# Attention and expert kernel on one core: the first pair's smallest scores get a visit and a load of their own, and the order is chosen anew

## The chip, the core and the metric

The kernel runs on one core of one Trainium2 chip. A core has TensorE for matrix products, which write to PSUM banks, VectorE, ScalarE and GpSimd for work on elements, and SyncE, which like ScalarE issues transfers (DMA). Each engine works through its own queue in order and waits on semaphores for the others. The metric is the time of one execution on the device in microseconds. The kernel before takes 539.85 us, the median of 3 runs (539.78 to 540.04).

## The reference

Local causal attention and a read from a memory are mixed by a gate for each head; the result goes through a two-layer network with a squared ReLU. B = 4, H = 8, S = 576, D = 64; 2304 tokens of 512 values, 2048 hidden units.

```python
scores = scale * q @ k.T            # causal, then softmax
local = softmax(scores) @ v
q_p = phi(q)                        # phi(x) = where(x > 0, x, exp(x) - 1) + 1
mem_out = (q_p @ M_prev) / ((q_p * z_prev).sum(-1) + 1e-6)
g = sigmoid(beta)                   # one for each head
attn = g * mem_out + (1 - g) * local
h = x @ w_in                        # x: attn, heads side by side
out = (s * relu(h) ** 2 + b) @ w_out
```

## The kernel before

Two heads make a pair; the sixteen pairs go through attention one after the other. The 576 queries of a head are cut into five tiles, 0 to 4 (the first has 64 rows, the others 128), whose causal widths are 64, 192, 320, 448 and 576 columns (`QW`). For each pair:

- SyncE loads q and k transposed (`load_qk`), q in rows (`qs`), z and the values with the memory (`V`). For pair 0 the q and k columns come in the chunks of `CHUNKS0`, and ScalarE's queue loads a second copy of q's first 64 columns.
- TensorE computes scores in visits, groups of tiles that share a buffer (`SCORES`, for pair 0 `SCORES0`). The buffers are `SB`, two tiles of two banks each, pool "S", and `TB`, four tiles of one bank, pool "T". A 32-bit product shows as two passes in the trace.
- VectorE adds the mask and takes the minimum (`red`, line 377), ScalarE exponentiates with a running sum (`ex`, line 383), VectorE inverts the sums, GpSimd or VectorE scales (`scale`, line 389). `phi` makes the memory's side from `qs`: ReLU and exponential on ScalarE, products with z on GpSimd or VectorE, and two `put`s (line 318) into the probabilities' tile `P`.
- TensorE transposes `P` in four banks (`bank`, line 468), ScalarE or VectorE copies them to `F` and `pt` (`copy`, lines 477 to 484), and TensorE multiplies by `V` (`second`, line 520). ScalarE and VectorE split the result into high and low parts (`xs`, `x4`, lines 541 and 542).

Between these stand the conversion of the weights w_in (`xa` to `w0H`, `w0L` and so on, lines 564 to 579) and, as soon as a batch's four pairs are there, the first layer's products (`mm1`, lines 586 to 588). When the pairs are through, the rest of the first layer and the whole second layer run on TensorE.

What sets the order: every step is added to a `Plan` with an engine, a cost, a rank and the pools that it takes and gives back. `ORDER` is a table with one number for each step; `deal` sorts each engine's steps by it, plays the queues against the costs, and emits the steps by their planned starts. `waits` then puts dummy products (`warm`) on the identity wherever the plan leaves TensorE a gap; `setup` puts `WARM` of them on zeros at the very start (line 247). Letters in tables choose an engine for each pair or tile: `RELU`, `ZMUL`, `PUTS`, `COPY`, `SCAL`, `HIGH`, `LOW`, `QL` (A ScalarE, D VectorE, P GpSimd). `HOME` chooses the pool for each early first-layer product. gin holds the gate's beta on its way through the sigmoid (lines 640 to 647), omg its complement.

## Time and profile before

| | before |
|---|---|
| median of 3 runs | 539.85 us |
| the profiled execution's own time | 539.81 us |
| its span, first to last instruction | 538.0 us |
| TensorE busy | 529.4 us, 98% |
| VectorE, ScalarE busy | 408.0 us, 405.6 us |
| GpSimd busy | 265.0 us |
| transfers | 81.51 MB |

The span is the time between the first and the last instruction of the program; what lies around it makes up the rest of the execution's time. Busy time is a union over an engine's instructions. An idle time that stands in brackets behind a row is the engine's wait just before the instruction, with the instruction that ended it. Instructions of one engine overlap a little where the next is taken up before the last has drained, so what an instruction costs its queue is read from its start to the next start. The ends of matrix products are modelled; their starts are recorded.

### The profile page before, as it was taken

To read this page: it belongs to the slowest core of one execution; us is meant where nothing else is said; L and a number is where in the kernel's file an instruction comes from. 1 tells how busy PE (TensorE), PEld (TensorE's weight loads), DVE (VectorE), ACT (ScalarE), POOL (GpSimd) and SP (SyncE) were. 2 spreads that over 40 slices of the span, in tenths; PEclk is the share of its full clock that TensorE was granted. 3 is DMA by queue.
4 is the path that set the end of the run, shared out by engine and by line. 5 is a ranking of instruction groups with operands and counts; after the bars stand their busy time and mean duration, and the time that the engine had idled before them with its cause. 6 is when DMAs were issued, how large, how long until landed. Compare 5 with 4: busy or idle time off the path is not lost.

```text
span 538.0 us, 11590 instructions
## 1 busy us (share of the span) xinstructions
PE 529.4 (98%) x4156; PEld 444.1 (83%) x4156; DVE 408.0 (76%) x1000; ACT 405.6 (75%) x895; POOL 265.0 (49%) x264
## 2 busy tenths in 40 slices
PE   8989999999999999999999999999999999999997
PEld 6767777777888778777788888899999998998996
DVE  5999999999877766545339897436798889889773
ACT  6999999988999546455336578879987887897840
POOL 3999544365784514121000000517768768768760
PEclk9999999999999999999999999999999999999999
DMA  7666668665514513212176756466353353452101
GB/s 224 183 174 188 231 213 256 210 175 190 160 67 143 182 62 114 78 60 84 40 277 239 252 193 214 147 217 195 115 169 110 122 176 95 141 163 90 39 30 40
DMA packets 56666, 81.51 MB, mean 152 GB/s; under 512 B 7584, under 2 KB 39072, under 8 KB 56608
## 3 DMA queue, kind: packets, MB, share of 16 engines
q1 hardware_dynamic: 54064, 78.63, 45.2%
q10 hardware_dynamic: 2544, 2.14, 1.2%
q8 instruction: 33, 0.54, 0.4%
q14 instruction: 25, 0.20, 0.1%
HBM read 57.15 MB, written 23.59 MB: 150 GB/s over the span
## 4 chain that ended last, share of the span: by engine, by line
PE 91%; ACT 6%; DVE 2%; DMA 1%; issue 0%; ACTq 0%; DVEq 0%
PE yps L868 12%; PE yps L872 11%; PE sb L520 7%; PE tb L586 7%; PE tb L587 6%; PE tb L588 6%; PE hps L586 5%; PE hps L587 5%; PE hps L588 5%; PE tb L468 5%; PE yps L871 5%; PE yps L870 5%; PE sb L364 4%; PE sb L370 2%; ACT P L383 2%; PE sb L586 2%
## 5 line engine op out<-in xcount | busy, mean ns | idle before, releaser
L383 ACT ACTIVATE P<-P,mn 128x64 f32<-128x64 f32 (+4 forms) x160 | 90.2, 571 | 15.2 <-DVE mn L377 15.2
L872 PE MATMUL yps<-rb,op 128*128 128x256 f32 x360 | 101.1, 281 | 0.0
L389 POOL TENSOR_SCALAR P<-P,sr,omg 128x192 f32<-128x192 f32 (+4 forms) x112 | 80.0, 726 | 36.0 <-ACT r L609 16.1
L377 DVE CUSTOM_DVE_ANT_0 P<-sb,mask 128x64 f32<-128x64 f32 (+4 forms) x160 | 73.1, 481 | 15.8 <-PE sb L364 12.8
L868 PE MATMUL yps<-rb,op 128*128 128x512 f32 x216 | 76.9, 396 | 0.0
L872 PEld LDWEIGHTS yps<-rb,op 128*128 128x128 f32 x360 | 67.9, 189 | 0.0
L848 POOL TENSOR_TENSOR sum<-src 128x512 f32<-128x512 f32 x10 | 12.9, 1294 | 104.3 <-ACT src L832 89.6
L856 POOL TENSOR_TENSOR op<-src,op 128x512 fp32r<-128x512 f32 x30 | 43.7, 1477 | 18.7 <-ACT op L855 18.6
L879 DVE TENSOR_TENSOR yu<-yu,yps 128x256 f32<-128x256 f32 x90 | 36.5, 414 | 20.3 <-PE yps L872 19.2
L868 PEld LDWEIGHTS yps<-rb,op 128*128 128x128 f32 x216 | 40.6, 188 | 9.0
L468 PEld LDWEIGHTS tb<-ident,P 64*128 64x128 f32 x928 | 36.1, 139 | 8.8 <-issue 4.1
L468 PE MATMUL tb<-ident,P 64*128 64x64 f32 x928 | 41.1, 226 | 1.6 <-DVE xs L542 0.7
L870 PE MATMUL yps<-rb,op 128*128 128x256 f32 x144 | 40.5, 281 | 0.0
L871 PE MATMUL yps<-rb,op 128*128 128x256 f32 x144 | 40.5, 281 | 0.0
L855 ACT CAST op<-src 128x512 fp32r<-128x512 f32 x50 | 30.4, 616 | 11.7 <-PE yps L872 8.8
L856 DVE TENSOR_TENSOR op<-sum,op 128x512 fp32r<-128x512 f32 x36 | 36.7, 1021 | 0.3 <-ACT op L855 0.2
L856 POOL TENSOR_TENSOR op<-w1H,op 128x512 fp32r<-128x512 f32 x24 | 34.9, 1481 | 0.0
L383 ACT ACTIVATION_READ_ACCUMULATOR P<-P,mn 128x1 f32 x160 | 32.8, 205 | 0.0
L370 PE MATMUL sb<-qk 64*128 64x288 f32 (+4 forms) x192 | 30.7, 415 | 1.9 <-DVE mn L377 1.7
L593 ACT ACTIVATE r<-hps 128x256 f32<-128x256 f32 x62 | 21.9, 386 | 13.5 <-DMA r_d<-r 9.4
L586 PE MATMUL tb<-xs,w0H 128*128 128x512 f32 x76 | 31.4, 413 | 0.0
L855 ACT CAST op<-sum 128x512 fp32r<-128x512 f32 x36 | 22.3, 619 | 11.9 <-PE yps L872 6.8
(177 smaller groups left out, 1618.5 us busy)
## 6 DMA issues: line engine op xcount, KB each, us to landing
r_d<-r SPq DMA_DIRECT2D x41, 256.0 KB, 2.4
src<-r_d SPq DMA_DIRECT2D x20, 512.0 KB, 4.5
qk<-in_qk_t_dram SPq DMA_DIRECT2D x15, 576.0 KB, 4.7
raw<-in_moe_w_out_dram SPq DMA_DIRECT2D x16, 512.0 KB, 6.5
w1H<-r_d SPq DMA_DIRECT2D x16, 512.0 KB, 4.5
xa<-in_moe_w_in_dram SPq DMA_DIRECT2D x12, 512.0 KB, 4.9
r_d<-r SPq DMA_DIRECT2D x48, 128.0 KB, 1.8
qs<-in_q_rows_dram SPq DMA_DIRECT2D x16, 320.0 KB, 3.4
```

Source lines behind the costliest of these rows:

```text
L377: nc.vector.tensor_tensor_reduce(P[:, j, PB[i] + 64:PB[i] + 64 + n], at(ps, j, o, n), m, -SCALE, 3.0e38, ALU.add, ALU.min, mn[:, j, i:i + 1])
L383: nc.scalar.activation(pt, pt, AF.Exp, scale=-1.0, bias=mn[:, j, i:i + 1], accum_out=sm[:, j, i, 0:1])
L389: e.tensor_scalar(pt, pt, sr[:, j, i:i + 1], omg[:, h:h + 1], ALU.mult, ALU.mult)
L468: nc.tensor.transpose(TB[ps[h]][:, o[h]:o[h] + 64], P[rs, j, c:c + 128], ident[rs, rs], tile_position=(64 * h, 0))
L586: nc.tensor.matmul(ps, lhsT=wH[:, p, fs], rhs=xs[:, 0], start=p == 0, stop=False)
L587: nc.tensor.matmul(ps, lhsT=wH[:, p, fs], rhs=xs[:, 1], start=False, stop=False)
L588: nc.tensor.matmul(ps, lhsT=wL[:, p, fs], rhs=xs[:, 0], start=False, stop=p == NP - 1)
L856: (nc.gpsimd if m in ONPOOL else nc.vector).tensor_sub(L, x, H.bitcast(F32))
L868: nc.tensor.matmul(tile, lhsT=H, rhs=B, start=f == 0, stop=False)
L870: nc.tensor.matmul(ps, lhsT=H, rhs=B[:, 0], start=f == 0, stop=False)
L871: nc.tensor.matmul(ps, lhsT=H, rhs=B[:, 1], start=False, stop=False)
L872: nc.tensor.matmul(ps, lhsT=L, rhs=B[:, 0], start=False, stop=f == KF - 1)
```

## The change

- `SCORES0` gives tile 0 of pair 0 a visit of its own, ahead of tile 1's. This visit takes two "T" banks, one for each head, and not an "S" buffer; `at`, `scores` and `red` get the pool as an argument for that. Each bank is given back by its own head's reduction.
- `CHUNKS0` gets a first chunk of 64 columns; the next 128 columns (64 to 192) are loaded from ScalarE's queue instead of SyncE's, behind the second copy of q's first 64 columns. gin's load, first on that queue before, now comes behind both.
- `WARM` goes from 7 to 6 products.
- The sums of tiles 0 and 1 are still inverted together, after tile 1's visit (`parts`).
- The tables of letters, `HOME` and `ORDER` are replaced. Pair 0's two puts go from VectorE to GpSimd.

```diff
 SCORES0 = (
-    ((0, 0, 64, 0), (1, 0, 192, 64)),
+    ((0, 0, 64, 0),),
+    ((1, 0, 192, 0),),
     ((2, 0, 320, 0),),
-CHUNKS0 = ((0, 192), (192, 448), (448, 576))
+CHUNKS0 = ((0, 64), (64, 192), (192, 448), (448, 576))
...
-    WARM, FILL = 7, (0, 0, 0, 0)
+    WARM, FILL = 6, (0, 0, 0, 0, 0)
...
-    PUTS = "DDPPDPDDPPPPPPPD"
+    PUTS = "PDPPPPDDPPPPPDPD"
...
         def load_qk(a, z):
-            nc.sync.dma_start(both[:, :, a:z], qk_t[b, p][:, :, a:z])
+            (nc.scalar if g == 0 and a == 64 else nc.sync).dma_start(both[:, :, a:z], qk_t[b, p][:, :, a:z])
...
-        def at(ps, j, o, n):
+        def at(ps, j, o, n, pool):
+            if pool == "T":
+                return TB[ps[j]][:, o:o + n]
             return SB[ps[j]][:, o:o + n] if len(ps) == 2 else SB[ps[0]][:, 512 * j + o:512 * j + o + n]
...
+            small = g == 0 and v == 0
+            pool = "T" if small else "S"
...
-            wide = v == len(visits) - 1
+            wide = small or v == len(visits) - 1
...
     ORDER = [
-        (one number for each step)
+        (one number for each step)
     ]
```

What the tables of letters and `ORDER` do is told by the engines' queues. ScalarE from its first instruction, before; `qk_106` holds pair 0's q and k, `P_120` its probabilities:

```order
L640 DMA gin<-in_beta_dram 128x8
L349 DMA qk_106<-in_qk_t_dram 128x64
L641 ACT_TABLE_LOAD
L641 ACTIVATE omg<-omg 128x8
L644 ACTIVATE gin<-gin 128x8
L383 ACTIVATE P_120,sm_116<-P_120,mn_114 128x64
L383 ACTIVATE P_120,sm_116<-P_120,mn_114 128x192
```

And now:

```order
L351 DMA qk_106<-in_qk_t_dram 128x64
L341 DMA qk_106<-in_qk_t_dram 128x2x128
L646 DMA gin<-in_beta_dram 128x8
L647 ACT_TABLE_LOAD
L647 ACTIVATE omg<-omg 128x8
L387 ACTIVATE P_120,sm_116<-P_120,mn_114 128x64 x2
L650 ACTIVATE gin<-gin 128x8
L387 ACTIVATE P_120,sm_116<-P_120,mn_114 128x192 x2
```

Two loads of q and k stand ahead of gin's, and gin's exponential stands between those of tile 0 (64 columns) and tile 1 (192 columns).

TensorE from its first product, before:

```order
L247 MATMUL tb_101<-xa 128x128 x7
L370 MATMUL sb_96<-qk_106 128x64 x2
L370 MATMUL sb_96<-qk_106 128x192 x2
L370 MATMUL sb_97<-qk_106 128x320 x2
L370 MATMUL sb_96<-qk_106 128x448 x2
```

And now:

```order
L248 MATMUL tb_101<-xa 128x128 x6
L374 MATMUL tb_98<-qk_106 128x64
L374 MATMUL tb_99<-qk_106 128x64
L374 MATMUL sb_96<-qk_106 128x192 x2
L374 MATMUL sb_97<-qk_106 128x320 x2
L374 MATMUL sb_96<-qk_106 128x448 x2
```

Tile 0's two scores have moved from the buffer that they shared with tile 1 to a bank each, and one product on zeros is gone.

ScalarE between the third pair's second product, whose result the casts of `xs` and `x` read, and the fourth pair's copies to `pt` and `F`, before; `P_120` now holds the fifth pair, `P_121` the fourth:

```order
L383 ACTIVATE P_120,sm_116<-P_120,mn_114 128x64
L566 ACTIVATE xa<-xa 128x256
L383 ACTIVATE P_121,sm_117<-P_121,mn_115 128x576
L295 ACTIVATE phr<-qs_110 128x640
L383 ACTIVATE P_120,sm_116<-P_120,mn_114 128x448
L541 CAST x_137<-tb_100 128x64
L541 CAST xs<-tb_101 128x256
L566 ACTIVATE xa<-xa 128x256
L541 CAST xs<-tb_100 128x256
L477 COPY pt<-tb_98 128x8x64
```

And now:

```order
L387 ACTIVATE P_120,sm_116<-P_120,mn_114 128x448
L387 ACTIVATE P_120,sm_116<-P_120,mn_114 128x192
L547 CAST x_137<-tb_100 128x64
L547 CAST xs<-tb_100 128x256
L547 CAST xs<-tb_99 128x256
L387 ACTIVATE P_120,sm_116<-P_120,mn_114 128x320
L572 ACTIVATE xa<-xa 128x256
L387 ACTIVATE P_120,sm_116<-P_120,mn_114 128x64
L581 CAST w0H<-xa 128x256
L483 COPY pt<-tb_98 128x8x64
```

Of the fifth pair's exponentials, two stood ahead of the fourth pair's copies, of 64 and 448 columns; now there are four, with one of 192 and one of 320.

## Rows read from the trace of the kernel before

**Rows 1.** Stretches: length, busy us (instructions) of PE, PEld, DVE, ACT, POOL; clock, DMA.

```profile
0.00:6.26 6.26, 4.98 (x26) 4.25 (x26) 0.89 (x7) 1.70 (x4) 2.08 (x12) 1.00 0.56 156
6.26:53.37 47.11, 43.41 (x492) 31.84 (x490) 45.55 (x182) 47.08 (x141) 40.67 (x55) 1.00 0.66 198
53.37:57.00 3.63, 3.57 (x37) 2.15 (x33) 3.63 (x11) 3.63 (x14) 0.98 (x1) 1.00 0.87 323
57.00:262.00 205.00, 205.00 (x1866) 159.87 (x1865) 156.84 (x484) 156.82 (x415) 91.18 (x107) 1.00 0.44 141
```

**Rows 2.** Timeline, 0.7 to 8 us, all engines: start us, us, engine, line, instruction.

```profile
0.72 1.34 SPq L340 DMA_DIRECT2D qk<-in_qk_t_dram  x2
0.73 0.39 ACTq L640 DMA_DIRECT2D gin<-in_beta_dram  x1
1.04 3.35 PE L247 MATMUL tb<-xa 128*128 128x128 f32 x14 [1.04 <-DVE omg L251]
1.16 0.44 ACTq L349 DMA_DIRECT2D qk<-in_qk_t_dram  x1
...
3.44 0.21 ACT L644 ACTIVATE gin<-gin 128x8 f32<-128x8 f32 x1 [0.30 <-DMA gin<-in_beta_dram]
...
4.64 1.67 PE L370 MATMUL sb<-qk 64*128 64x64 f32 x12 [0.25 <-DMA qk<-in_qk_t_dram]
...
5.93 0.22 DVE L377 CUSTOM_DVE_ANT_0 P<-sb,mask 128x64 f32<-128x64 f32 x1 [1.84 <-PE sb L370]
...
6.26 0.35 ACT L383 ACTIVATE P<-P,mn 128x64 f32<-128x64 f32 x1 [2.61 <-DVE mn L377]
...
6.91 1.02 PE L370 MATMUL sb<-qk 64*128 64x448 f32 x4 [0.61 <-DVE mn L377]
...
7.98 0.62 DVE L377 CUSTOM_DVE_ANT_0 P<-sb,mask 128x448 f32<-128x448 f32 x1 [0.30 <-PE sb L370]
```

**Rows 3.** Line 247: engine, operation, count, duration in ns (least, median, most), first and last start.

```profile
L247 PE MATMUL tb<-ident x38: 275/275/377, 7.9 to 43.7; 128*128 128x128 f32 x38
```

**Rows 4.** Timelines of TensorE, ScalarE and GpSimd, 50 to 54 us.

```profile
50.54 0.71 PE L468 MATMUL tb<-ident,P 64*128 64x64 f32 x16 [0.18 <-POOL P L318]
...
52.57 1.08 PE L370 MATMUL sb<-qk 64*128 64x320 f32 x7
53.71 0.76 PE L520 MATMUL tb<-F,V 128*64 128x320 f32 x4
...
51.77 1.23 ACT L479 COPY F<-tb 128x512 f32<-128x512 f32 x2
52.73 0.54 ACT L484 COPY F<-tb 128x256 f32<-128x256 f32 x1
53.00 0.65 ACT L481 COPY F<-tb 128x384 f32<-128x384 f32 x1
...
51.04 0.78 POOL L318 TENSOR_TENSOR P<-qs,nrm 128x256 f32<-128x256 f32 x1
```

**Rows 5.** Loads of q and k: queue, count, KB each, median us to landing.

```profile
qk<-in_qk_t_dram SPq DMA_DIRECT2D x1, 128.0 KB, 4.2
qk<-in_qk_t_dram ACTq DMA_DIRECT2D x1, 32.0 KB, 3.3
```

**Rows 6.** Groups by shape, TensorE, 4.5 to 6.4 us: busy us, mean ns, idle before.

```profile
L370 PE MATMUL sb<-qk 64*128 64x64 f32 x4 | 0.7, 437 | 0.2 <-DMA qk<-in_qk_t_dram 0.2
```

**Rows 7.** Timeline of ScalarE, 6.6 to 9.8 us.

```profile
6.60 0.44 ACT L383 ACTIVATE P<-P,mn 128x192 f32<-128x192 f32 x1
...
7.04 0.33 ACT L383 ACTIVATE P<-P,mn 128x64 f32<-128x64 f32 x1
...
9.21 0.55 ACT L383 ACTIVATE P<-P,mn 128x320 f32<-128x320 f32 x1
...
9.75 0.55 ACT L383 ACTIVATE P<-P,mn 128x320 f32<-128x320 f32 x1
```

**Rows 8.** Timeline of GpSimd, its first work on pair 0.

```profile
10.24 1.54 POOL L305 TENSOR_TENSOR phr<-qs,z 128x640 f32<-128x640 f32 x1 [7.47 <-DVE sr L440]
```

More of the change, by code (lines that the diff above doesn't have):

```diff
@@ L272, in attention_moe_kernel @@
     RSR, WL = 0.6, 3
-    RELU = "AAAAAAAADADAAADP"
-    ZMUL = "PPPDDPDDDDPPDDDD"
-    PUTS = "DDPPDPDDPPPPPPPD"
-    COPY = ["AAAD", "AAAD", "AAAA", "AAAA", "AAAA", "AAAA", "AAAA", "AADA", "ADAA", "AAAA", "DAAA", "DDAD", "DDDA", "ADAD", "ADAA", "ADDA"]
-    SCAL = ["PPPPP", "PPPPP", "PPPPP", "PPPPP", "PPPPD", "DPPPD", "PPDPD", "PPPDP", "PPPDP", "DPPPP", "PPPDP", "PDDDP", "PDDPD", "DPDPD", "PPDPP", "DDDDD"]
-    HIGH, LOW = "PPAPAAPPAAAAAAAAAAPA", "PDPDDPPDDDPDPDDPDDDD"
-    QL = "DDDDDDDDPDDPPPPD"
+    RELU = "AAAAAAAADAAADDAD"
+    ZMUL = "PPPDDPDDDPPPDDDP"
+    PUTS = "PDPPPPDDPPPPPDPD"
+    COPY = ["AAAD", "AAAD", "AAAA", "AAAA", "AAAA", "AAAA", "AAAA", "AADA", "DDAA", "AAAA", "DAAD", "DAAA", "AAAA", "DADA", "ADAA", "DDAA"]
+    SCAL = ["PPPPP", "PPPPP", "PPDPP", "PPPPP", "PPPPD", "PPDPP", "DPPPD", "PPPDD", "DPPDP", "DPPPP", "DPPPP", "PDDPD", "DDDDD", "PDPDD", "DPDPD", "PDPDD"]
+    HIGH, LOW = "APPAPAPAAAAAAAAAAAAA", "PDPDDDPDDDPDPDDPDDDD"
+    QL = "DDDDDDDDPDPPPDPD"
     PARTS = "3232332223222222"
@@ L345, in attention @@
         for v, (a, z) in enumerate(chunks):
-            add("SP", 0.9 if g else 0.6, lambda a=a, z=z: load_qk(a, z), (r0 if g else 0) - 4.0 + 0.01 * v, writes=[("qk", u, v)],
-                bytes=(400000, 190000, 200000)[v] if g == 0 else 380000 if g == 1 else 128 * 8 * (z - a) + 32768, slack=2 if g else 1)
+            on = "ACT" if g == 0 and v == 1 else "SP"
+            add(on, 0.9 if g else 0.45 if v == 1 else 0.6, lambda a=a, z=z: load_qk(a, z), (r0 - 4.0 if g else -9.5 if v == 1 else 0) + 0.01 * v, writes=[("qk", u, v)],
+                bytes=(130000, 130000, 230000, 200000)[v] if g == 0 else 380000 if g == 1 else 128 * 8 * (z - a) + 32768, slack=(2 if g else 1) if on == "SP" else 0)
         if g == 0:
@@ L350, in attention, with scores @@
         phi(g)
-        def at(ps, j, o, n):
+        def at(ps, j, o, n, pool):
+            if pool == "T":
+                return TB[ps[j]][:, o:o + n]
             return SB[ps[j]][:, o:o + n] if len(ps) == 2 else SB[ps[0]][:, 512 * j + o:512 * j + o + n]
         fast = g >= FAST
-        def scores(group, ps):
+        def scores(group, ps, pool):
             for i, c0, n, o in group:
@@ L370, in scores, with red @@
                     nc.tensor.matmul(
[L371 removed]
+                        at(ps, j, o, n, pool), lhsT=qk[rs, 128 * i:128 * i + 128], rhs=qk[rs, S + 64 + c0:S + 64 + c0 + n],
                         start=True, stop=True, tile_position=(64 * j, 0))
[L374 removed]
+        def red(i, j, o, ps, pool):
             n = QW[i]
@@ L377, in red @@
             nc.vector.tensor_tensor_reduce(
-                P[:, j, PB[i] + 64:PB[i] + 64 + n], at(ps, j, o, n), m, -SCALE, 3.0e38, ALU.add, ALU.min,
+                P[:, j, PB[i] + 64:PB[i] + 64 + n], at(ps, j, o, n, pool), m, -SCALE, 3.0e38, ALU.add, ALU.min,
                 mn[:, j, i:i + 1])
@@ L414, in attention @@
                 cost = sum(n + 32 for _, _, n, _ in group) / 800 + 0.05
-            add("PE", cost, lambda group=group, ps=ps: scores(group, ps), r,
-                [(x, u, k) for x in ("qh", "ql") for k in range(2)] if fast else [("qk", u, k) for k in range((1, 2, 2, 3)[v] if g == 0 else 1)] + [("qk", 0, "d")] * (g == 0),
-                [("sc", g, v), "visit"], take=[(ps, "S")] * (2 if v == len(visits) - 1 else 1), mode="row")
-            wide = v == len(visits) - 1
+            add("PE", cost, lambda group=group, ps=ps, pool=pool: scores(group, ps, pool), r,
+                [(x, u, k) for x in ("qh", "ql") for k in range(2)] if fast else [("qk", u, k) for k in range((1, 2, 3, 3, 4)[v] if g == 0 else 1)] + [("qk", 0, "d")] * (g == 0),
+                [("sc", g, v), "visit"], take=[(ps, pool)] * (2 if small or v == len(visits) - 1 else 1), mode="row")
+            wide = small or v == len(visits) - 1
             if g == 0 and FILL[v]:
@@ L426, in attention @@
                     last = k == len(tiles) - 1 and (wide or j == 1)
-                    add("DVE", RED[i], lambda i=i, j=j, o=o, ps=ps: red(i, j, o, ps), r + 0.1 + 0.01 * k - UR,
+                    add("DVE", RED[i], lambda i=i, j=j, o=o, ps=ps, pool=pool: red(i, j, o, ps, pool), r + 0.1 + 0.01 * k - UR,
                         [("sc", g, v)] + ([("rd", g, v, h, q) for h in ((j,) if wide else range(2)) for q in range(len(tiles))] if last else []),
-                        [("p", u, i, j), ("mn", u, i, j), ("rd", g, v, j, k)], give=[(ps, j if wide else 0, "S")] if last else ())
+                        [("p", u, i, j), ("mn", u, i, j), ("rd", g, v, j, k)], give=[(ps, j if wide else 0, pool)] if last else ())
                     add("ACT", EXP[i], lambda i=i, j=j: ex(i, j), r + 0.15 + 0.01 * k, [("mn", u, i, j)],
@@ L630, in attention_moe_kernel @@
     LEFT = 7
-    HOME = "TTTTTTTTTTSTTTTTTTTTTTSSSTTTTTTTTTTTSTSSS"
+    HOME = "TTTTTTTTTTSTTTTTTTTTTTSTSTTTTSSTTTTTSTSSS"
     JOIN = "b0b00000b000a0bb"
```

6 lines of the change are left out of this document (2 added, 4 removed), and 102 rows, old and new, of the table ORDER.

## The prediction

> **What bounds the kernel now.** I read the stretches first [rows 1]. From 57 to 262 us TensorE is busy 205.00 of 205.00 us, and what follows is the second half of the network on the same engine. So nothing that the first pairs do can be won back after 57 us: what is early or late there moves the end by as much. The idle time of TensorE lies ahead of that point: 6.26 - 4.98, 47.11 - 43.41 and 3.63 - 3.57, together 5.04 us. Products without use fill part of what would be further gaps: 14 passes on zeros (7 products of two passes) from 1.04 us [rows 2] and 38 on the identity [rows 3].
>
> The second column to read is ScalarE. From 6.26 us, where it starts its first exponential, to 53.37 us, where it has issued the last copy of the fourth pair, it is busy 47.08 of 47.11 us [rows 1]. VectorE (45.55) and GpSimd (40.67) have gaps there. So the head of the kernel is one ScalarE queue with a start time and a length. The fourth pair's second product (line 520) starts at 53.71 us: 0.06 us after the visit ahead of it has ended, and 0.71 us after the last copy began, which takes 0.65 [rows 4]. That start is the milestone. Ahead of it TensorE has the same useful work in both orders; behind it the same again, with 71 changes between row-tiled, column-tiled and full products in either order. The time of the kernel is then the milestone plus a constant.
>
> Profiled, the kernel took 539.81 us (span 538.0); the median of the runs is 539.85, 0.04 more. I add to 539.81.
>
> **The start.** Today [rows 2]: the zero products run from 1.04 to 4.39 us; the first scores wait for q and k until 4.64; VectorE's first reduction starts at 5.93, the first exponential at 6.26, 0.33 later. Three edits move this.
>
> Dummies: 14 passes take 3.35 us, 0.239 each, so 12 end near 1.04 + 2.87 = 3.91. That is the earliest start of the scores.
>
> Loads: the second copy of q's first 64 columns, 32 KB, leaves ScalarE's queue at 0.73 instead of 1.16 [rows 2], as gin's load now comes last there. It landed 3.3 us after its issue [rows 5] and released the scores; moved by 0.43 it lets them start at 4.21. The other load that they need shrinks from 192 columns to 64. Between 3.91 and 4.64 (no gain) I take 4.1, nearest to the shifted copy, a little ahead of it because fewer bytes share the engines with it.
>
> Own visit: today's first reduction reads a tile that the matmuls of tiles 0 and 1 write, with one wait for all of them. Now tile 0 has two banks to itself, and the reduction needs only the four 64-column passes, busy 0.7 us [rows 6]. The hand-over I take from the 448-column visit: it ends at 6.91 + 1.02 = 7.93, its reduction starts at 7.98 [rows 2], 0.05 us. New: 4.1 + 0.70 + 0.05 = 4.85, + 0.33 = **5.18 for the first exponential, 1.08 us earlier**. The ends: 3.91 gives 4.99 (1.27 earlier), 4.64 gives 5.72 (0.54 earlier).
>
> Here a rule speaks against the edit of the loads. The row: SyncE spends 1.34 us on issuing its first two loads [rows 2], so a load moved to ScalarE's queue can spare the next one some 0.67 us of issue; that the issue sets the landing no row shows. The Trainium skill, page "DMA: Bandwidth & Descriptors", section "Issuing engines are not separate DMA queues", says that loads started from several engines run on the same 16 DMA engines and interleave, and that issuing from more of them saves only the time of issue. By it my 0.11 us for fewer bytes beside the copy would be void, since the same bytes follow at once from the other queue, and the sum below would be 540.03 instead of 539.92.
>
> **The ScalarE queue.** Now its length to the milestone. I counted what stands ahead of the fourth pair's last copy in each order. Copies, casts, conversions and the 64-, 448- and 576-column exponentials agree in number. The new order has three instructions more: gin's exponential, which today runs at 3.44 in idle time (0.21 us [rows 2]) and now stands between those of tiles 0 and 1; and a 192- and a 320-column exponential of the fifth pair, which today come after the copies. From start to next start a 192 takes 0.44 us (6.60 to 7.04), a 320 takes 0.54 (9.21 to 9.75) [rows 7]. Sum 0.21 + 0.44 + 0.54 = **1.19 us longer**. Without gaps in ScalarE the milestone is 53.71 - 1.08 + 1.19 = 53.82 and the time 539.81 + 0.11 = **539.92 us**; with the ends of the start 539.73 and 540.46. The earlier start is spent on work moved ahead of the critical copies. Behind them that work is gone, but there TensorE waits for nobody, so its absence earns nothing.
>
> **The rest.** gin's load and the table load go back by one or two issues of about 0.4 us each on ScalarE's queue; they are wanted at 5.2 us, and today were through by 3.65, so more than a microsecond covers them. On SyncE a load of weights goes behind the third pair's q and k, which wait for the first pair's last scores; the conversion that reads it stands behind some 15 us of ScalarE's queue, which covers it; uncovered, each microsecond costs one. Products on the identity: one fewer in all, two passes of 0.275 us [rows 3]. They fill waits, so at ScalarE's pace they give nothing, and 0.55 us if TensorE set the milestone. GpSimd's queue up to the fourth pair's last put trades two 320-column scales for one pair of puts and stays near 41.6 us. Tables of later pairs swap engines where VectorE and ScalarE have 48 us to spare of 205 [rows 1]: nothing, while no wait of TensorE appears; one that does costs its length.
>
> **Rivals.**
> (a) *ScalarE's queue is not what counts*, and the earlier start reaches the end whole, as if the fifth pair's two exponentials ran in a hole. For it: gin and these two are work that has no urgency. Against it: 47 us without a hole today, and the engine works in order. Time 539.81 - 1.08 = 538.73, or 538.54 with the early end.
> (b) *GpSimd sets the milestone, slower than before.* Pair 0's puts (0.78 us for the smaller, by a later pair's row [rows 4]) now stand on GpSimd ahead of the two 576-column scales that the pair's last transposes need. From GpSimd's first multiply at s the last put of the fourth pair ends 41.58 us later (10.24 [rows 8] to 51.82 [rows 4]); then come the transposes of two banks (0.71 + 0.05), the three copies ahead of the last (1.23) and the last copy (0.71) [rows 4]: s + 44.28. Against 53.82 it decides from s = 9.54. For it: the multiply starts at 10.24 today, behind VectorE's chain. Against: that chain should be about a microsecond earlier. If s stays 10.24 the milestone is 54.52, the time 539.81 + 0.81 = 540.62, and every pause of GpSimd comes on top.
> (c) *A hole opens behind tile 0.* Tile 1's columns ride second on ScalarE's queue. Landing as late as 128 KB did on SyncE's (4.2 us after issue [rows 5], so near 1.2 + 4.2 = 5.4), they give scores at 5.4, a reduction at 5.4 + 0.7 + 0.05, and an exponential at least the 0.33 us of today behind it, at 6.48. ScalarE is through with tile 0 (twice 6.26 to 6.60) and gin at 5.18 + 0.68 + 0.21 = 6.07: 0.41 idle, 540.33.
> (d) *The scores start no earlier*, both loads still landing near 4.5: 540.46, the late end above.
> (e) *A new wait of TensorE* somewhere in the 205 us that have none: 541 and more.
>
> **How the numbers follow.** Forecast, ScalarE's queue with an earlier start, 539.6 to 540.3: 0.52. (a) 0.12, (b) 0.14, (c) and (d) together 0.14, (e) 0.08. A measurement of this kernel tells 0.2%, 1.08 us, from no change: below 538.77 is faster, above 540.93 slower. Faster: (a) where nearly all of the start arrives, 0.09. Slower: (e), and (b) or (c) with pauses on top, 0.13. Within: 0.78. The likeliest time is 539.9. The range 538.9 to 541.0 leaves out the better part of (a) and most of (e).
>
> **What would show it.** Right: the first exponential near 5.2, ScalarE again without a wait of over 0.1 us to its last copy for the fourth pair, this queue about 48.3 us long, the product of line 520 within 0.3 us of 53.8, and no wait of TensorE behind it. (a) shows as that product starting near 52.7; (b) as transposes waiting for GpSimd's puts; (c) as ScalarE waiting between tiles 0 and 1; (d) as scores at 4.6; (e) as TensorE's waits after 57 us. The reading is wrong altogether if the milestone and the end move by different amounts.

## The result and the profile after

The changed kernel takes **544.17 us**, the median of 4 runs (543.25 to 545.03), beside 539.90 for the kernel before in the same comparison. The ratio is 1.0079, 95% interval 1.0061 to 1.0096. It is slower, and the time lies 4.3 us above the forecast and 3.2 above the upper end of its range. The profiled execution took 543.96 us with a span of 542.2.

A first look at the stretches of [rows 1] in the kernel after (columns: stretch, length, then the busy time with the count of instructions of TensorE, its weight loads, VectorE, ScalarE and GpSimd, granted clock, DMA share, GB/s):

```profile
6.26:53.37 47.11, 40.53 (x440) 29.89 (x442) 45.04 (x171) 44.39 (x134) 37.12 (x51) 0.96 0.59 184
...
57.00:262.00 205.00, 204.97 (x1857) 159.69 (x1858) 159.62 (x491) 161.03 (x427) 87.69 (x101) 1.00 0.46 146
```

ScalarE, busy 47.08 of 47.11 us before, is now busy 44.39: it has lost 2.69 us to waits. TensorE is 2.88 us less busy there and saw a lower clock for a while (0.96 on average). Behind 57 us the long full stretch is as full as before.

The start of this execution came as planned. The timeline after that answers [rows 2] (columns of a timeline: start, duration, engine, line, operation, output<-inputs, count, and in brackets the engine's wait just before with its releaser):

```profile
3.91 0.69 PE L374 MATMUL tb<-qk 64*128 64x64 f32 x4
...
4.75 0.22 DVE L381 CUSTOM_DVE_ANT_0 P<-tb,mask 128x64 f32<-128x64 f32 x1 [3.74 <-PE tb L374]
...
5.23 0.35 ACT L387 ACTIVATE P<-P,mn 128x64 f32<-128x64 f32 x1 [1.23 <-DVE mn L381]
```

The first exponential stands at 5.23 instead of 6.26 us. But the milestone, the fourth pair's second product (line 526 now, 520 before), went the other way, from 53.71 to 57.03:

```profile
57.03 0.76 PE L526 MATMUL tb<-F,V 128*64 128x320 f32 x4
```

Between the two I followed ScalarE's holes. Four are longer than 0.1 us: 0.82 us ahead of 11.59, 1.20 ahead of 21.69, 0.15 ahead of 44.99 and 0.52 ahead of 50.55. They make up the 2.69. The two long ones have one picture, in the timelines of all engines:

```profile
9.32 1.54 POOL L306 TENSOR_TENSOR phr<-qs,z 128x640 f32<-128x640 f32 x1 [6.53 <-DVE qs L302]
...
9.66 1.23 DVE L653 TENSOR_SCALAR omg<-omg 128x8 f32<-128x8 f32 x1
...
10.80 0.74 DVE L381 CUSTOM_DVE_ANT_0 P<-sb,mask 128x576 f32<-128x576 f32 x1
...
11.59 0.78 ACT L387 ACTIVATE P<-P,mn 128x576 f32<-128x576 f32 x1 [0.82 <-DVE mn L381]
...
11.61 2.11 PE L374 MATMUL sb<-qk 64*128 64x448 f32 x16 [1.27 <-DVE mn L381]
...
19.64 1.87 DVE L574 SCALAR_TENSOR_TENSOR xa<-xa 128x256 uint32<-128x256 uint32 x1
19.68 1.55 POOL L306 TENSOR_TENSOR phr<-qs,z 128x640 f32<-128x640 f32 x1
...
21.69 0.35 ACT L387 ACTIVATE P<-P,mn 128x64 f32<-128x64 f32 x1 [1.20 <-DVE mn L381]
```

Read it from GpSimd's multiply with z (line 306). At 9.66 VectorE begins a step on 8 elements (omg, the gate's complement); it takes 1.23 us and ends at 10.89, as the multiply ends at 10.86. At 19.64 a step of the weights' conversion takes 1.87 us and ends at 21.51, after the next multiply's 21.23. Behind each stand the reductions that ScalarE and, for its score banks, TensorE wait for. So a short VectorE step was held until GpSimd's long one was through. In the kernel before neither stands in such a place: line 647, the same step of omg, runs ahead of the multiply, which starts at 10.24 [rows 8], and line 568, the same step of the conversion as line 574 now, first starts at 22.73, 1.89 us behind the end of the second multiply, and takes 0.41.

```profile
8.53 0.17 DVE L647 TENSOR_SCALAR omg<-omg 128x8 f32<-128x8 f32 x1
```

Two further losses lie elsewhere. TensorE waits 1.92 us, until 41.52, for a copy of ScalarE (first fence below). From 43.11 to 46.52 its granted clock is 0.50, the 1.2 GHz level (two windows in the columns above, then one group of shapes: busy us, mean ns of one):

```profile
41.52 0.49 PE L474 MATMUL tb<-ident,P 64*128 64x64 f32 x9 [1.92 <-ACT pt L483]
```

```profile
38.00:41.50 3.50, 1.60 (x24) 1.05 (x24) 3.50 (x11) 3.50 (x14) 1.79 (x3) 1.00 0.62 178
43.10:46.50 3.40, 3.40 (x40) 2.77 (x40) 2.70 (x9) 3.25 (x9) 3.15 (x5) 0.50 0.84 307
```

```profile
L474 PE MATMUL tb<-ident,P 64*128 64x64 f32 x32 | 1.9, 312 | 0.0
```

A transpose takes 312 ns there; in the kernel before, from 47.2 to 52.6 us, 58 of the same took 231 each. And at the start of the second layer, a place that the forecast never looked at, TensorE waits for the last ReLU of the first layer:

```profile
359.29 0.66 ACT L599 ACTIVATE r<-hps 128x256 f32<-128x256 f32 x2
...
360.00 0.50 PE L874 MATMUL yps<-rb,op 128*128 128x512 f32 x1 [0.80 <-ACT r L599]
```

Before, the same product starts at 356.11 without a wait:

```profile
356.11 0.40 PE L868 MATMUL yps<-rb,op 128*128 128x512 f32 x1
```

The 4.15 us that the span grew add up from starts alone: -1.03 to the first exponential; +2.97 from there to the first pair's product (24.32 - 5.23 = 19.09 against 22.38 - 6.26 = 16.12: the holes 0.82 and 1.20, gin's exponential 0.21, and 0.74 not assigned); +1.38 to the fourth pair's (32.71 against 31.33); and +0.83 behind it (542.18 - 57.03 = 485.15 against 484.32), of which 0.80 is the new wait.

### The profile page after: what moved, and what is told of

It is laid out like the page before. It is cut to its first block, busy times and chain, and to the rows that moved or that the text cites. A ratio compares the mean times of both kernels' runs of the same rounds, so it can differ in the third digit from the quotient of the medians.

```text
span 542.2 us, 11581 instructions
## 1 busy us (share of the span) xinstructions
PE 529.8 (98%) x4152; PEld 444.6 (82%) x4152; DVE 409.2 (75%) x1000; ACT 409.1 (75%) x903; POOL 259.7 (48%) x256
## 4 chain that ended last, share of the span: by engine, by line
PE 91%; ACT 4%; DVE 2%; issue 1%; POOL 1%; ACTq 0%; DVEq 0%
PE yps L874 12%; PE yps L878 11%; PE sb L526 7%; PE tb L592 6%; PE tb L593 5%; PE tb L594 5%; PE hps L592 5%; PE hps L593 5%; PE hps L594 5%; PE tb L474 5%; PE yps L877 5%; PE yps L876 5%; PE sb L368 4%; PE sb L374 3%; ACT P L387 2%; PE sb L592 2%
## 5 line engine op out<-in xcount | busy, mean ns | idle before, releaser
L393 POOL TENSOR_SCALAR P<-P,sr,omg 128x320 f32<-128x320 f32 (+4 forms) x104 | 72.6, 709 | 59.4 <-DVE sr L447 52.3
L387 ACT ACTIVATE P<-P,mn 128x448 f32<-128x448 f32 (+4 forms) x160 | 89.7, 566 | 8.6 <-DVE mn L381 8.2
L862 DVE TENSOR_TENSOR op<-sum,op 128x512 fp32r<-128x512 f32 x36 | 35.4, 986 | 1.3 <-ACT op L861 1.2
L592 PE MATMUL tb<-xs,w0H 128*128 128x512 f32 x80 | 33.0, 412 | 0.0
L483 ACT COPY pt<-tb 128x512 f32<-128x512 f32 x48 | 27.3, 593 | 6.6 <-PE tb L474 6.3
```

The lines of the kernel that those rows point to most:

```text
L387: nc.scalar.activation(pt, pt, AF.Exp, scale=-1.0, bias=mn[:, j, i:i + 1], accum_out=sm[:, j, i, 0:1])
L393: e.tensor_scalar(pt, pt, sr[:, j, i:i + 1], omg[:, h:h + 1], ALU.mult, ALU.mult)
L592: nc.tensor.matmul(ps, lhsT=wH[:, p, fs], rhs=xs[:, 0], start=p == 0, stop=False)
L862: (nc.gpsimd if m in ONPOOL else nc.vector).tensor_sub(L, x, H.bitcast(F32))
```

## The experiments

All kernels compute everything. The edits of the order are single numbers of `ORDER`, which move the named step in its engine's queue. The milestone and the rest behind it, read from each profiled execution:

| kernel | median us | ratio to before, 95% | first exponential | milestone | end minus milestone | runs at a clock of 0.997 or less |
|---|---|---|---|---|---|---|
| before | 539.9 to 540.2 | | 6.26 | 53.71 | 484.3 | 0 of 75 |
| after | 544.17 | 1.0061 to 1.0096 | 5.23 | 57.03 | 485.1 | 3 of 4 |
| e1_omg_early | 543.58 | 1.0051 to 1.0075 | 5.23 | 55.67 | 485.9 | 2 of 5 |
| e2_conv_late | 542.58 | 1.0033 to 1.0057 | 5.44 | 55.53 | 485.0 | 0 of 5 |
| e3_both | 542.78 | 1.0037 to 1.0061 | 5.23 | 54.54 | 487.9 | 1 of 6 |
| e4_before_omg_late | 541.21 | 1.0016 to 1.0040 | 5.98 | 54.55 | 484.3 | 3 of 12 |
| e5_after_banks | 542.93 | 1.0037 to 1.0063 | 5.24 | 56.29 | 484.0 | 3 of 5 |
| e6_before_banks | 542.10 | 1.0026 to 1.0054 | 5.98 | 53.99 | 485.7 | 0 of 5 |
| e7_both_banks | 541.82 | 1.0014 to 1.0036 | 5.49 | 55.43 | 484.0 | 0 of 7 |
| e8_exps_back | 541.75 | 1.0018 to 1.0040 | 5.58 | 55.88 | 484.3 | 0 of 7 |
| e9_letters | 543.80 | 1.0054 to 1.0078 | 5.47 | 56.65 | 484.2 | 4 of 6 |
| e10_late_start | 542.29 | 1.0024 to 1.0049 | 6.51 | 56.45 | 484.0 | 2 of 5 |
| e11_start_alone | 539.51 | 0.9987 to 1.0008 | 5.46 | 53.57 | 484.3 | 0 of 12 |
| e12_start_mended | 539.42 | 0.9989 to 1.0011 | 5.17 | 53.14 | 484.4 | 0 of 12 |

The last column counts a kernel's timed executions by their mean granted clock. The profile of the changed kernel, with its 3.41 us at 0.50, has a mean of 0.996, and that of e3, with 3.41 us too, 0.997; the twelve profiles without such a stretch have 0.999 or 1.000. So a median compares executions with the low clock and without it where the counts differ, and what one edit is worth is better read from the starts in the profiles.

### e1_omg_early: the first meeting taken away

```diff
-    ]
+    ]; ORDER[6] = 33.1; ORDER[7] = 33.2
```

The steps of lines 652 and 653 go ahead of VectorE's step of line 302, whose result GpSimd's multiply reads, and so ahead of that multiply.

> The changed kernel, with VectorE's two small steps for omg (lines 652 and 653) put ahead of its step of line 302, so that they are through before GpSimd's long multiply (line 306) begins. In the changed kernel line 653 starts 0.34 us after that multiply, takes 1.23 us and ends 0.03 us after it. Theory 1, the two engines shut each other out: line 653 takes about 0.17, the 576-column reductions start near 9.9 instead of 10.8, ScalarE's hole of 0.82 us ahead of the first 576-column exponential closes to under 0.2, TensorE's wait of 1.27 us at 10.34 shrinks to under 0.5; everything up to 19 us comes 0.8 earlier. If line 574 meets the next multiply as before, the time falls by 0.8, to about 543.3. Theory 2, the loss is TensorE's lower clock (43.1 to 46.5 us at half): the holes may close, but the time falls only if the low clock goes too, then by 1.3 to 1.7. Theory 3, ScalarE's longer queue and not the holes: no change, 544.2.

```profile
8.82 0.17 DVE L653 TENSOR_SCALAR omg<-omg 128x8 f32<-128x8 f32 x1
...
15.23 1.41 POOL L319 TENSOR_TENSOR P<-qs,nrm 128x384 f32<-128x384 f32 x2
...
15.59 1.20 DVE L573 TENSOR_SCALAR xa<-xa 128x256 uint32<-128x256 uint32 x1
...
19.20 1.55 POOL L306 TENSOR_TENSOR phr<-qs,z 128x640 f32<-128x640 f32 x1
...
19.74 1.29 DVE L574 SCALAR_TENSOR_TENSOR xa<-xa 128x256 uint32<-128x256 uint32 x1
```

The step takes 0.17 us by itself, and the hole of 0.82 is gone. The kernel gained only 0.6 us: a conversion step met GpSimd's puts (line 319) at 15.59 instead, taking 1.20 us, and ScalarE's second hole stayed at 1.20. The milestone came 1.36 earlier in the profile, but only 0.49 of that had come by the first pair's product (23.83 instead of 24.32); 0.93 is the stretch from the second pair's product to the fourth's (21.52 instead of 22.45), where this execution kept the full clock. Of the 1.36 us, 0.78 went to a longer wait at the second layer (1.57 instead of 0.80).

### e2_conv_late: the second meeting taken away

```diff
-    ]
+    ]; ORDER[89] = 115.5
```

The conversion step of line 574 goes behind two reductions.

> The changed kernel, with VectorE's step of line 574 (first of the two merges of the first weight piece) put behind the two reductions of line 381 that follow it. In the changed kernel it starts at 19.64, 0.04 us ahead of GpSimd's second multiply (19.68 to 21.23), and takes 1.87 us where others take 0.41; ScalarE then waits 1.20 us for the reduction behind it and TensorE 1.22. Theory 1, the engines shut each other out: the reductions run at once, both waits fall under 0.3, the time falls by about 1.2 to 543.0, by up to 1.4 more if the low clock goes with the wait of 1.92 us at 39.6. Theory 2 (clock): the time moves only with the clock. Theory 3 (longer queue): 544.2.

```profile
19.89 1.56 POOL L306 TENSOR_TENSOR phr<-qs,z 128x640 f32<-128x640 f32 x1
...
20.68 0.75 DVE L381 CUSTOM_DVE_ANT_0 P<-sb,mask 128x576 f32<-128x576 f32 x1
...
21.36 0.42 DVE L574 SCALAR_TENSOR_TENSOR xa<-xa 128x256 uint32<-128x256 uint32 x1
```

The reduction takes 0.75 us beside GpSimd's multiply, which is its normal time; it reads its scores from PSUM. The conversion step behind it takes 0.42 instead of 1.87. ScalarE's hole fell from 1.20 to 0.11 and the first one stayed; from the first exponential to the first pair's product it is 17.99 us instead of 19.09. The median fell by 1.6 us. That is more than the hole; none of e2's five runs has the low clock, which three of the changed kernel's four have.

### e3_both: the two moves together

The two edits above in one kernel.

> Both moves of steps in the changed kernel together: lines 652 and 653 ahead of line 302, and line 574 behind the two reductions. Theory 1: holes of 0.82 and 1.20 us in ScalarE's queue both gone, the product of line 526 of the fourth pair at 55.0 or earlier instead of 57.03, the time 544.2 - 2.0 = 542.2; if with them the stretch at half clock goes, another 1.4: 540.8; if also the wait of 0.80 us at 359.2 goes, 540.0, which is the prediction's number. Theory 2: 544.2 unless the clock is up throughout. Theory 3: 544.2.

ScalarE has one hole of over 0.1 us left before 57 us, 0.44. The milestone is 54.54, 2.49 earlier than in the changed kernel, and still 0.83 later than before. The median, 542.78, is not below that of e2. In the profiled execution, the slowest of the six (544.19), the wait at the second layer was now 1.96 us; behind it, from 359.74 on, the granted clock was 0.50 for 3.41 us. ScalarE's queue is almost full again, as the windows under "Why the prediction was wrong" show, but it is no longer the only thing that is late. The chain that ended last (start, duration, piece) leads from VectorE over GpSimd's scales to the transposes:

```profile
45.76 0.09 DVE nrm L309
...
45.85 0.41 POOL w0H L579
46.26 1.24 POOL P L393 x2
...
47.62 2.87 POOL P L393 x4
```

Early in the kernel another wait shows. TensorE is through with the first pair before the second pair's q and k are there:

```profile
10.98 2.11 PE L374 MATMUL sb<-qk 64*128 64x448 f32 x16 [0.87 <-DMA qk<-in_qk_t_dram]
```

### e4_before_omg_late: the meeting put into the kernel before

```diff
-    ]
+    ]; ORDER[7] = 43.5
```

> The kernel before, with VectorE's small step of line 647 (omg) put where it falls into GpSimd's first multiply (10.24 to 11.78), ahead of the 576-column reductions, as in the changed kernel. Nothing else of the change. Theory 1: line 647 takes over 1 us instead of 0.17 and ends with the multiply, at 11.8; the reductions start at 11.8 instead of 10.56, the first 576-column exponential at 12.5 instead of 11.60; ScalarE's hole of 0.9 us goes to the product of line 520 (54.6) and to the end: 540.8. Theories 2 and 3: no change, 539.9.

```profile
9.96 1.54 POOL L305 TENSOR_TENSOR phr<-qs,z 128x640 f32<-128x640 f32 x1 [7.19 <-DVE sr L440]
...
10.22 1.31 DVE L647 TENSOR_SCALAR omg<-omg 128x8 f32<-128x8 f32 x1
...
12.23 0.78 ACT L383 ACTIVATE P<-P,mn 128x576 f32<-128x576 f32 x1 [0.82 <-DVE mn L377]
```

One small step moved in the kernel before makes the same picture, 1.31 us for eight elements and a hole of 0.82 at ScalarE. The milestone is 0.84 later and the median 1.1 us higher. The converse holds: the meeting alone makes the hole, without the rest of the new order. Three of its twelve runs have the low clock, too.

### e5_after_banks and e6_before_banks: the wait at the second layer

When attention is through, the last results of the first layer rotate through all eight banks in the order of `BANK`, which is sorted by the last use of each buffer in attention. `HOME` and `ORDER` decide that last use. The changed kernel's order is [6, 7, 5, 4, 2, 3, 0, 1], that of before [6, 4, 5, 7, 0, 1, 2, 3]. There are 39 results; the last one lies at index 6 of the list, bank 0 after the change and bank 2 before. The second layer's first product takes bank 0.

```diff
-    BANK = sorted(range(8), key=lambda k: last("S", k // 2) if k < 4 else last("T", k - 4))
+    BANK = [6, 7, 5, 4, 0, 1, 2, 3]
```

The kernel before got the reverse, `BANK = [6, 4, 5, 7, 2, 3, 0, 1]`, in e6.

> The changed kernel with one line changed: the order in which the eight PSUM banks go round in the stage of 262 to 360 us (line 915, sorted by last use in the stage ahead) is written out as 6, 7, 5, 4, 0, 1, 2, 3 instead of 6, 7, 5, 4, 2, 3, 0, 1, so that the last of its 39 results lies in bank 2, as in the kernel before, and not in bank 0. Theory B, the bank: the first product of line 874 goes to bank 0 and in the changed kernel waits for ScalarE to read the last result out of it (0.80 us at 359.2); the wait disappears, the time falls by 0.8, to 543.4. Rival, the stores: ScalarE is late there because its buffers wait for stores of results, whatever the bank; the wait stays and the time with it, 544.2.

> The kernel before with the same line the other way round: banks 6, 4, 5, 7, 2, 3, 0, 1 instead of 6, 4, 5, 7, 0, 1, 2, 3, so that the last result of that stage lies in bank 0. Nothing else is changed. Theory B: the first product of line 868 (356.11) waits until ScalarE has read the last result, which starts 0.53 after it and takes 0.39: a wait of 0.9 us that the kernel before does not have, and 540.9. Rival, the stores: no wait, 540.0.

In e5 TensorE has no wait behind 262 us, and the rest behind the milestone falls from 485.1 to 484.0; the median falls by 1.24. Ahead of 262 us e5 is the changed kernel unaltered, and shows one thing more. It has the same long wait of TensorE, and the clock stays up behind it (timeline, then the window in the columns above):

```profile
41.74 0.49 PE L474 MATMUL tb<-ident,P 64*128 64x64 f32 x9 [1.91 <-ACT pt L483]
```

```profile
43.00:46.50 3.50, 3.47 (x54) 2.77 (x50) 3.47 (x13) 3.50 (x11) 3.34 (x6) 1.00 0.91 311
```

From the second to the fourth pair's product it is 21.47 us (34.82 to 56.29), in the changed kernel's profile 22.45 (34.58 to 57.03). So 0.98 us of that profile's milestone is the low clock, and another execution of the same work need not have it.

In e6 the wait appears:

```profile
357.58 0.50 PE L868 MATMUL yps<-rb,op 128*128 128x512 f32 x1 [1.13 <-ACT r L593]
```

It lasts 1.13 us; the rest behind the milestone grows by 1.4 and the median by 2.0. Both directions agree on the cause. The 0.9 us of e6 beyond the wait are partly a milestone 0.28 later; the remainder I did not trace.

### e7_both_banks: all three causes taken away

The moves of e1 and e2 and `BANK = [6, 4, 7, 5, 0, 1, 2, 3]`.

> The changed kernel with all three: lines 652 and 653 early, line 574 late, and bank 0 not last. Theories 1 and B together: the product of line 526 of the fourth pair at 54.54 as with the two moves alone, from there to the end 484.32 us as in the kernel before, so a span of 538.9 and a time of 540.6. What is left over 540.0 is then the head alone, 54.54 against 53.71. If the wait at 359 stays, 542.0 to 542.8.

The median is 541.82, 2.35 us below the changed kernel and still 1.7 above the kernel before; the 540.6 expected were missed, as the milestone was 55.43 and not 54.54. Nothing is left behind the milestone (484.0). The profiled execution has a meeting that e3, with the same order, has not:

```profile
15.44 1.40 POOL L319 TENSOR_TENSOR P<-qs,nrm 128x384 f32<-128x384 f32 x2
...
15.80 1.19 DVE L573 TENSOR_SCALAR xa<-xa 128x256 uint32<-128x256 uint32 x1
```

In e3 the same two stand as follows:

```profile
15.07 1.45 POOL L319 TENSOR_TENSOR P<-qs,nrm 128x384 f32<-128x384 f32 x2
...
15.74 0.31 DVE L573 TENSOR_SCALAR xa<-xa 128x256 uint32<-128x256 uint32 x1
```

In the row of e3, which holds two puts, VectorE's step begins 0.67 us behind the row's start, in e7 0.36 us. In e3 it takes its normal time. So whether a step meets another depends on a few tenths of a microsecond, by which the two executions differ already at the first exponential (5.23 and 5.49).

### e8_exps_back: the two exponentials that the forecast priced

```diff
-    ]; ORDER[6] = 33.1; ORDER[7] = 33.2; ORDER[89] = 115.5
+    ]; ORDER[6] = 33.1; ORDER[7] = 33.2; ORDER[89] = 115.5; ORDER[531] = 370.1; ORDER[529] = 370.2
```

On top of e7, the fifth pair's 192- and 320-column exponentials go behind the fourth pair's last copies.

> As the one with all three, and in ScalarE's queue the 192-column and the 320-column exponential of the fifth pair that the change put ahead of the fourth pair's copies go behind the last of them. TensorE's order is the same. The prediction's term: they cost 0.44 + 0.54 us of the queue; without them the product of line 526 of the fourth pair comes 0.98 earlier, at 53.6, and the time is 539.6. If GpSimd's scales or TensorE itself set that product, it moves by less: 0 to 0.5, and 540.1 to 540.6.

From the first pair's product to the fourth's it is 31.86 us, in e7 31.91: the two are worth 0.05 us and not 0.98. Ahead of that the two profiles differ for another reason (TensorE's products on the identity took 421 ns each up to about 10 us in e8 and 275 in e7, and ScalarE waited 1.28 us at 12.39), so the milestones of the table are not set side by side. The median is 0.07 lower, less than the runs differ among themselves; both values that were expected, 539.6 and 540.1 to 540.6, were missed. Where they had stood, ScalarE now waits for transposes, which wait for GpSimd:

```profile
51.71 0.59 ACT L483 COPY pt<-tb 128x512 f32<-128x512 f32 x1 [0.52 <-PE tb L474]
...
51.87 0.71 PE L474 MATMUL tb<-ident,P 64*128 64x64 f32 x16 [0.17 <-POOL P L393]
```

### e9_letters: two letters given back

```diff
-    SCAL = ["PPPPP", "PPPPP", "PPDPP",
+    SCAL = ["PPPPP", "PPPPP", "PPPPP",
...
-    HIGH, LOW = "APPAPAPAAAAAAAAAAAAA", "PDPDDDPDDDPDPDDPDDDD"
+    HIGH, LOW = "APPAPAPAAAAAAAAAAAAA", "PDPDDPPDDDPDPDDPDDDD"
```

On top of e7, VectorE is relieved of the steps of two letters, which GpSimd did before the change. My theory was that VectorE's queue holds the milestone.

> As the one with both moves of steps and bank 0 not last, and two letters of the tables set back to those of the kernel before: the two 320-column scales of the third pair and one subtraction of the sixth weight piece go from VectorE back to GpSimd. With the holes of ScalarE gone, the chain that ended last runs from 32 to 46 us through VectorE without a pause, and from the second product of line 526 to the third it takes 11.4 us where the kernel before takes 10.65. Theory, VectorE is what is late there: it has 0.8 + 0.35 us less to do, the third and the fourth product of line 526 come 0.7 earlier, the time is 541.1. Rival, GpSimd: it gets 1.9 us more, in a stretch where it waits 1.8 and 1.1 us for VectorE; if that is not enough room, the time rises, to 543.

```profile
35.87 3.95 POOL L393 TENSOR_SCALAR P<-P,sr,omg 128x192 f32<-128x192 f32 x4
...
39.26 0.52 PE L474 MATMUL tb<-ident,P 64*128 64x64 f32 x10 [1.83 <-POOL P L393]
```

It fell. The milestone is 1.22 later. The median is 2.0 higher, but four of the six runs have the low clock, and the two without it took 542.69 and 542.71, 0.9 above the median of e7. TensorE waits 1.83 us for a scale of GpSimd's. With these letters the third pair's scales on GpSimd come last, as the rival had it. In this new order the two letters belonged together with the order.

### e10_late_start: what the start is worth

```diff
-    WARM, FILL = 6, (0, 0, 0, 0, 0)
+    WARM, FILL = 9, (0, 0, 0, 0, 0)
```

On top of e7, three products of zeros more delay the first scores. My theory here was that the start no longer lies on the path.

> As the one with both moves of steps and bank 0 not last, with nine products of zeros ahead instead of six: the first scores start 1.2 to 1.4 us later, the first exponential near 6.5, later than in the kernel before (6.26). All else stands in the same order. Theory, the early start is not on the chain: the second pair's scores wait for that pair's q and k, which land at 10.85, and for VectorE; they start 0 to 0.6 us later and the time is 541.8 to 542.4, or earlier where the products bring the high clock sooner. The prediction's step, a start that comes through whole: 543.1.

```profile
6.51 0.35 ACT L387 ACTIVATE P<-P,mn 128x64 f32<-128x64 f32 x1 [2.51 <-DVE mn L381]
```

The first exponential is 1.02 later than in e7 and the milestone, 56.45 instead of 55.43, is 1.02 later too. In this pair of profiles the start comes through whole. The times do not say so: the medians differ by 0.47 and the fastest runs by 0.66, and 542.29 lies in the range of my theory and not near the 543.1 of a start that comes through whole. How much of a later start reaches the end stays open between 0.5 and 1.0 us for 1.02.

### e11_start_alone and e12_start_mended: the start without the new order

e11 has the first pair's edits (own visit, loads, six products) and for all other steps the order, letters and `HOME` of the kernel before; only the two small steps for gin on VectorE go behind tile 1's reductions, since gin lands later now. e12 has in addition gin's exponential behind tile 0's two, and one conversion step (line 576) behind a reduction that it had delayed.

```diff
...
-    PUTS = "PDPPPPDDPPPPPDPD"
...
+    PUTS = "DDPPDPDDPPPPPPPD"
...
-    HOME = "TTTTTTTTTTSTTTTTTTTTTTSTSTTTTSSTTTTTSTSSS"
+    HOME = "TTTTTTTTTTSTTTTTTTTTTTSSSTTTTTTTTTTTSTSSS"
...
```

> The first pair's part of the change alone: tile 0's scores in a visit and a first load of their own, the next 128 columns from ScalarE's queue, six products of zeros; every other step stands in the order of the kernel before, with its letters, homes and banks (the two small steps for gin on VectorE go behind the reductions of tile 1, since gin now lands later). Theory: the start is worth about what it brings, and the new order lost it. The first exponential near 5.2 (6.26 before), no new meeting of VectorE and GpSimd, the product of line 526 of the fourth pair 0.4 to 1.0 earlier than 53.71 (0.4 if the second pair's q and k, which landed at 10.85 in the changed kernel, hold its scores), the span after it 484.3: 539.1 to 539.7, faster than the kernel before by 0.1 to 0.2%. Rival: the steps that now come 1 us earlier meet GpSimd's long ones too, and the time is 540.0 to 541.5.

> The first pair's part alone in the order of before, as in the run ahead, with two steps moved. Gin's exponential goes behind tile 0's two, as in the changed kernel: in the run ahead ScalarE waited 1.35 us for gin's load and took it 0.2 us ahead of the first exponential. And VectorE's last merge of a weight piece, which in the run ahead met GpSimd at 50.94 (0.83 us instead of 0.41) ahead of a reduction for which TensorE then waited 0.42 us at 52.09, goes behind that reduction. Theory: the wait of 0.42 goes, the start comes 0.2 earlier, the fourth pair's product of line 526 is at 53.0 to 53.2 instead of 53.57, the time 539.0 to 539.2 against 540.0 for the kernel before. Rival: VectorE meets GpSimd elsewhere, and the time stays at 539.5 or rises to 540.5.

In e11 two new waits show up, for gin's load at ScalarE, and 0.42 us at 52.51 behind a conversion step that met a GpSimd product of 0.90 us begun at 50.59:

```profile
5.34 0.21 ACT L650 ACTIVATE gin<-gin 128x8 f32<-128x8 f32 x1 [1.35 <-DMA gin<-in_beta_dram]
...
50.94 0.83 DVE L576 SCALAR_TENSOR_TENSOR xa<-xa 128x256 uint32<-128x256 uint32 x1
...
52.51 0.81 PE L374 MATMUL sb<-qk 64*128 64x320 f32 x4 [0.42 <-DVE mn L381]
```

In e12 the step stands behind the reduction and takes half the time:

```profile
50.97 0.74 DVE L381 CUSTOM_DVE_ANT_0 P<-sb,mask 128x576 f32<-128x576 f32 x1
...
51.64 0.41 DVE L576 SCALAR_TENSOR_TENSOR xa<-xa 128x256 uint32<-128x256 uint32 x1
```

e12's first exponential is 1.09 earlier than in the kernel before, its milestone 0.57 and its span 0.5. Its median, 539.42, is the lowest of all kernels here, but the ratio's interval, 0.9989 to 1.0011, holds 1: against the kernel before it is no difference that these runs can tell. The same goes for e11, of which 0.1 to 0.2% were expected. Seven of e12's twelve runs lie between 539.08 and 539.43, the others between 540.6 and 541.4. The kernel before falls apart too: six of its seventeen runs beside e12 lie between 539.40 and 539.56, the others between 539.90 and 541.64. Why they do stays open.

## Why the prediction was wrong

- **The start** was right, in part by luck: 5.18 forecast, 5.23 measured; scores at 3.91 instead of 4.1, the reduction at 4.75 instead of 4.85. In this execution the scores began as the products of zeros ended, and the landing of the loads did not decide. In e2, e7, e8 and e9, with the same loads, they waited for q and k until 4.15 to 4.32 (e7's row is below), and the first exponential stood at 5.44 to 5.58; the kernel before has 6.26 in its profile, but e4 and e6, with its start, have 5.98. So by the profiles the start is worth between 0.4 and 1.0 us (5.98 less 5.58, 6.26 less 5.23), and the 4.1 of the forecast cannot be told from the 4.21 of the weighed rule on issuing queues. That a microsecond at the start is a microsecond at the milestone, on which the sum rests, e10's profile bears out (1.02 for 1.02) and its median only in part (0.47).

```profile
4.20 0.69 PE L374 MATMUL tb<-qk 64*128 64x64 f32 x4 [0.22 <-DMA qk<-in_qk_t_dram]
```

- **"Without gaps in ScalarE the milestone is 53.82"** is the step that failed. ScalarE had gaps of 2.69 us, and the milestone was 3.21 late. The windows below (first exponential to milestone; ScalarE's busy time, clock, DMA) are of the kernel before, the changed one and e3. The queue itself was forecast 1.19 us longer; it is 1.63 longer in the changed kernel and 1.39 in e3, so that term was a little small. The gaps, which the sum put at nothing, are 2.75 and 0.50. I compared the count of instructions on each engine's queue in the two orders, but not what VectorE and GpSimd do at the same time. The first holes come from two meetings of theirs (e1, e2, and the converse in e4). In the kernel before none of these two stood there. The program's plan marks other VectorE steps as meeting GpSimd's (the argument `port=True`, at lines 302 and 573 to 576 among others), but line 653 is not marked; I had read the order without that.

```profile
6.26:53.71 47.45, 47.42 (x142) 1.00 0.66 197
...
5.23:57.03 51.80, 49.05 (x147) 0.97 0.61 189
...
5.23:54.54 49.31, 48.81 (x147) 1.00 0.64 199
```

- The Trainium skill, page "SBUF — State Buffer", section "Who interferes with whom", says that the two engines share a pair of ports under an exclusive lock; that a VectorE `tensor_scalar` can enter a two-port mode in which whichever of the two engines comes second stands still for the other's whole instruction; that a VectorE instruction with two inputs in SBUF contends with a GpSimd instruction that reads SBUF; and that one with a single SBUF input outside that mode is free. The trace agrees: 1.23 us against 0.17 for line 653, 1.87 against 0.42 for line 574, and 0.75 for the 576-column reduction from PSUM in the same place; a reduction (line 446, at 9.50) and a reciprocal (line 447, at 9.57) inside the first multiply took 0.16 and 0.17 us and were not held. It says also that whoever issues first gets the pair; line 574's record begins 0.04 us ahead of GpSimd's at 19.64, and it was still the one that waited. The records' starts do not tell the order at that distance.
- **"The time of the kernel is then the milestone plus a constant"** failed too, by 0.83 us, as the prediction had named for its own refutation. The constant holds for the 205 us that I checked, and not at 359 us, where the new `HOME` and `ORDER` had changed the order of the banks. I costed `HOME` nowhere. Rival (e) had such a wait, but in the wrong stretch; e5 and e6 show the cause from both sides.
- **The fifth pair's two exponentials**, 0.44 and 0.54 in the sum, measured 0.05 together (e8). In e8 ScalarE waits 0.52 and 0.32 us for transposes where the two had stood, so shortening its queue alone gains nothing there. gin's 0.21 does lie ahead of the first pair's work; it was not measured by itself.
- **Rival (b)**, GpSimd setting the milestone, is nearest to what remains with the meetings gone: in e3 the chain ends over GpSimd's scales, e9 loads GpSimd with one pair more and loses 2.0 us. But its condition was another: it was to start late at 10.24, and the multiply started at 9.32 (9.58 in e3, just above the 9.54 from which it was to decide). And the prediction let GpSimd's queue stay near 41.6 us; from the first multiply to the end of the fourth pair's last put it takes 42.32 in e3 (9.58 to 51.90) and 41.41 in e12 (9.35 to 50.76).
- **The lower clock** stands in no step. It is worth 0.98 us of the profiled execution, by e5, which runs the same instructions up to there at the full clock. It follows a wait of TensorE of 1.9 us that the kernel before does not have there. Three of the changed kernel's four runs have a mean clock of 0.996 and spans of 542.2 to 543.2 us, the fourth 0.999 and 541.5, so it is in the median of 544.17 as well. None of the 75 runs of the kernel before has it, but three of e4's twelve do, where one step was moved: so the new order as a whole is not needed for it. Why it falls in one execution and not in the next no run shows.

What of the 4.3 us is shown. From starts in the profiles, the 4.15 us of span divide so: -1.03 the start; +1.74 the two meetings (from the first exponential to the first pair's product 19.09, in e3 17.35); +1.23 more on that stretch (e3's 17.35 against 16.12); +1.38 from there to the fourth pair's product, of which 0.98 is the low clock (e5); +0.83 behind it, of which 0.80 is the wait for the bank (e5, e6). The medians give 0.6, 1.6 and 1.2 by single edits (e1, e2, e5) and 2.35 by all three together (e7). These are not clean prices: other waits take a removed one's place, and the low clock, in three of the changed kernel's four runs and none of e7's, is counted in with each.

The remaining 1.7 us of e7 over the kernel before come with the new order, letters and `HOME` of the rest, since e12 keeps the start and gives these back, and is 2.4 us faster than e7. Where they lie is read from e3 and e12 only: 0.8 us up to the first pair's product (22.58 against 21.79) and 0.6 from there to the milestone (31.96 against 31.35; the chain over GpSimd). The wait of 0.87 us for q and k in e3 explains little of the 0.8: the product behind it starts at 10.98, and its like in e12 at 10.80.

```profile
10.80 2.11 PE L374 MATMUL sb<-qk 64*128 64x448 f32 x16 [0.35 <-DVE sr L447]
```

No experiment took these two losses away singly, so their cause stays open.

## What to carry to other kernels

Before forecasting a new order from the lengths of the engines' queues, lay VectorE's and GpSimd's starts beside each other: a VectorE step of the kinds that were held here (a `tensor_scalar` in SBUF, or a step that reads two SBUF tensors) can cost the rest of a long GpSimd instruction in which it begins, and it delays everything behind it in VectorE's queue. Reductions and reciprocals were not held. A hole at ScalarE or TensorE is then read backwards to the one instruction that is several times longer than its like. A table that is derived from the order, here that of the banks, belongs to the change, however far behind in the program it is used. And before an edit's price is read from two medians, count in how many runs of each the granted clock fell.
